# Seven block products for eight: q and k of one 512-token chunk, with their token sums, and the gate folded into v's products

## The chip, the cores and the metric

One core of a Trainium2 chip. The engines work side by side, each through its own instructions in order: TensorE (PE; its weight loads are shown as PEld), VectorE (DVE), ScalarE (ACT), GpSimd (POOL) and SyncE (SP), which here issues the DMAs. They wait for each other by semaphores. The metric is device time in microseconds.

## The reference

Input x is 2048 tokens by 448. The result mixes local attention (16 heads of 28, each token looking at 8 keys, 2 apart) with a two-layer perceptron (1792 hidden, squared ReLU), by a gate per token:

```
g = sigmoid((x * gate_w).sum(-1, keepdims=True))
qkv = x @ wqkv                      # q, k, v: 448 columns each
logits = einsum(q, k[idx]) * scale  # idx = pos - 0, 2, .. 14; masked below 0
a = softmax(logits) @ v[idx] @ wo
h = relu(x @ w1 + b1);  b = (h * h) @ w2 + b2
return g * a + (1 - g) * b
```

All is float32, and all of it is computed.

## The kernel before

**Products.** A float32 matrix is split into a high part, rounded to the type that TensorE reads (`fp32r`), and a low part, the rest: ScalarE writes the high part, VectorE subtracts it (`split_full`). A product is three passes: high by high, high by low, low by high. The contraction of 448 is three blocks of 128 and one of 64. Nearly all products run as two of 64 rows side by side (`side_by_side`, line 186): one on rows 0-63 into one PSUM bank, one on rows 64-127 into another. After a bank's products on one half of the rows it changes to the other half. At this *turn* a one-element write into the bank (VectorE's memset, line 196, in `turn`) waits for the products so far, and the next products wait for it.

**q, k, v.** The tokens come in four chunks of 512 (four tiles of 128). Chunk 0 goes through `qkv_first`, chunks 1 to 3 through `qkv_two`, twice each, two tiles at a time: 63 pairs of products, q of one tile beside k of the other. Its last tuple of steps says after how many pairs a turn is issued and after how many a bank is copied out:

```
[(24, [], (q0, k1)), (36, [], (q1, k0)), (42, [], (v0, v1)), (45, [(0, t0, q0), (1, t1, k1)]),
 (51, [], *beside[:1]), (54, [(0, t1, q1), (1, t0, k0)]), (57, [], *beside[1:]),
 (63, [(2, t0, v0), (2, t1, v1)])]
```

So a bank turned after 24 pairs is written again from pair 36, one turned after 36 from pair 45, one turned after 42 from pair 54. ScalarE copies a finished bank to a staging tile (line 205; three buffers), SP stores that to `q_d`, `k_d` or `v_d` in DRAM (line 211). Chunks 0 and 1 are the first half of the tokens for attention, 2 and 3 the second.

**Attention** works in eight units (two halves, four groups of four heads) from `q_d`, `k_d`, `v_d`. GpSimd multiplies (lines 335 and 342; 8 and 8 instructions a unit) into one of four product buffers (`pp`), and VectorE sums each up (lines 336, 350), at least two products behind.

**The perceptron** takes the chunks in the order 3, 0, 1, 2; its first products lie among the last of chunk 3's v. w1 and w2 are split in pieces. The later pieces of w1 (2 and 3) and w2 are split by `split_copied`: ScalarE writes the high part (line 514) and copies the raw rows to a PSUM bank that is used for that alone (line 515), VectorE subtracts (line 520), 1.3 us later in the kernel's clock; the next copy waits for that. Chunk 3's x tiles are copied to the tiles that the perceptron reads (line 736).

**What sets the order.** The order of instructions is written by a planner inside the kernel. `clock["pe"]` goes on by 203 ns for every pair of 448 columns (`advance`). Work is queued with a due time (`when`: absolute; `at`: from now; `soon`: 1.5 us from now) and is issued on its engine once the clock has passed it; within one `advance` all that is due comes first, then attention's steps (2.3 us for each product with k, the first 17 us after chunk 1's end). Each engine then works through its list in that order, at whatever time the chip gets there. A tile or bank that is used again makes its first writer wait for the last reader of what it held, a DMA's landing included; of the buffers of one kind the one that was given back first is used first.

**The gate.** VectorE multiplies each chunk's raw x by `gate_w` as four instructions (`z_product`), transposes and sums (`z_sums`); the sums go through DRAM once (`z_store`, `z_load`, `z_last`).

Of the kernel before, what the change touches and what calls it, by code (L numbers as in the profile page):

```python
# [14 lines left out]
P = 128  # L15
# [3 lines left out]
G = 4  # L19
# [4 lines left out]
NQ = D + 2  # L24
NZ = 64
NP = 512
# [31 lines left out]
def gated_mix_kernel(ctx: ExitStack, tc: tile.TileContext, xT, wqkv, w1, w2, wo, b1, b2, out):  # L58
# [11 lines left out]
    z_d = tc.dram_tile([P, NZ], F32, name="z_d")  # L70
# [10 lines left out]
    w1h = const.tile([P, 3, F], F32R, name="w1h")  # L81
    w1l = const.tile([P, 3, F], F32R, name="w1l")
# [8 lines left out]

    xpool = ctx.enter_context(tc.tile_pool(name="xpool", bufs=1))
# [5 lines left out]
    zg = smallp.tile([P, 6, NS], F32, name="zg")  # L98
    zt, gt, g1t = zg[:, 0:2], zg[:, 2:4], zg[:, 4:6]
# [36 lines left out]
    def x_split(raw, x, k):  # L136

        split_full(raw[:, k], x.h[k], x.l[k])
# [15 lines left out]
    wqh = ap.tile([P, 3, NP + 2 * D], F32R, name="wqh")  # L154
    wql = ap.tile([P, 3, NP + 2 * D], F32R, name="wql")

    w7h = ap.tile([P, NP + D], F32R, name="w7h")
    w7l = ap.tile([P, NP + D], F32R, name="w7l")
# [3 lines left out]
    nc.gpsimd.memset(halo0, 0.0)  # L162

    stage = {}

    def block(b):

        o = (0, NP, NP + D)[b]
        return slice(o, o + D)
# [29 lines left out]
    def qkv_evacuate(pt, c, tl, b):  # L199
        par, t = c // 2, (c % 2) * 4 + tl  # L200
        first = (b, t // 2) not in stage
        if first:
            stage[b, t // 2] = xap.tile([P, G, 2, C], F32, tag="stage", name=f"st{c}_{tl}_{b}", bufs=ST_BUFS)
        st = stage[b, t // 2]
        nc.scalar.activation(st[:, :, t % 2], pt[:, :D].rearrange("p (g c) -> p g c", g=G), AF.Copy)  # L205
        if not first:
            stage.pop((b, t // 2))
            t0 = t - t % 2
            dst, off = ((q_d, 0), (k_d, HALO), (v_d, HALO))[b]
            dd = dst[par, :, off:off + SP].rearrange("g (p s) c -> p g s c", s=NS)[:, :, t0:t0 + 2]  # L210
            nc.sync.dma_start(dd.rearrange("p g s c -> p g (s c)"), st.rearrange("p g s c -> p g (s c)"))
# [9 lines left out]
    def last(x, acc, tl, b):  # L221

        sl = slice(tl * P, tl * P + P)
        n = block(1) if b == 2 else slice(0, D)
        h, l = w7h[:, n], w7l[:, n]
        return [(acc, x.x7[:, sl], h), (acc, x.x7[:, sl], l), (acc, x.x8[:, sl], h)]

    def accs(c, b, tls, tags):
        return [Acc(t, f"qkv{c}_{tl}_{b}", D) for t, tl in zip(tags, tls)]
# [60 lines left out]


# [101 lines left out]
    def gates(par):  # L393

        e = smp.tile([P, 32], F32, tag="e", name=f"e{par}")[:, :NS]
        nc.scalar.activation(e, zt[:, par], AF.Exp, scale=-1.0)
# [127 lines left out]
    def w1_piece(i, dt, gap):  # L524
# [4 lines left out]
        sl = slice(i * n, (i + 1) * n)  # L529

        def part(k):
            if k < 3 and i > 1:
                split_copied(dt + k * gap, raw[:, k, :n], [(slice(0, P), slice(0, n), w1h[:, k, sl], w1l[:, k, sl])])
                return
            if k < 3:
                split_full(raw[:, k, :n], w1h[:, k, sl], w1l[:, k, sl], soon)
# [12 lines left out]
            for rows, cols, hi, lo in parts:  # L549
                split_full(raw[rows, 3, cols], hi, lo, soon)  # L550
# [10 lines left out]
    def x_load(c):  # L561
        raw = raw_tile(f"xraw{c}")
# [22 lines left out]
    def h_full(x, acc, f, ks):  # L585
        fs = slice(f * P, f * P + P)
        return sum((three(acc, w1h[:, k, fs], w1l[:, k, fs], x.h[k], x.l[k]) for k in ks), [])
# [11 lines left out]
    def h_turn(accs, f):  # L599
        touch(w1h[:, 2].rearrange("p (f n) -> p f n", n=P)[:, f:f + 2, 0:1])  # L600
        for a in accs:
            a.rows = None
# [34 lines left out]
    raws = [raw_tile("wqraw0")]  # L637
    rx = raw_tile("xraw0")
    for k in range(4):
        if k < 3:  # L640
            nc.sync.dma_start(raws[0][:, k, :NQ], wqkv[0, :, k])
        else:
            for b, rows in ((0, slice(0, 64)), (1, slice(64, P))):
                nc.sync.dma_start(raws[0][rows, k, :NQ], wqkv[b, rows, k])
# [3 lines left out]
    for b, tag in ((1, "k"), (2, "v")):  # L648
        raw = attp.tile([P, 3, D], F32, tag=tag, name=f"wqraw{b}")
        for k in range(3):  # L650
            nc.sync.dma_start(raw[:, k], wqkv[b, :, k, :D])
        raws.append(raw)
    raw7 = attp.tile([P, D], F32, tag="q", name="wqraw7")
    nc.sync.dma_start(raw7, wqkv[2, :, 3, :D])
    x = x_tiles(0, xap)
    for k in range(3):
        nc.scalar.activation(wqh[:, k, :D], raws[0][:, k, :D], AF.Copy)
# [7 lines left out]
        nc.vector.tensor_sub(wql[:, k, :D], raws[0][:, k, :D], f32(wqh[:, k, :D]))  # L665
        for cols in halves:
            nc.vector.tensor_sub(x.l[k][:, cols], rx[:, k, cols], f32(x.h[k][:, cols]))
    split_full(raws[0][:, 3, :D], w7h[:, :D], w7l[:, :D])
    split_x78(rx[:, 3], x.x7, x.x8)

    zs = smp.tile([P, 3, NZ], F32, tag="lg", name="zs")
    zu = xcp.tile([P, CH], F32, tag="zu", name="zu")
    zpart, zall, gw = zs[:, 0], zs[:, 1], zs[:, 2, 0:4]
    nc.vector.tensor_copy(gw, raws[0][:, :, D])

    def z_product(raw, k):

        r = slice(0, P if k < 3 else 64)
        if k:
            nc.vector.scalar_tensor_tensor(zu[r], raw[r, k], gw[r, k:k + 1], zu[r], op0=ALU.mult, op1=ALU.add)  # L680
        else:
            nc.vector.tensor_scalar_mul(zu, raw[:, 0], gw[:, 0:1])

    def z_sums(c):

        nc.vector.transpose(zu, zu)
        nc.vector.tensor_reduce(
            zpart.rearrange("p (b c t) -> p c t b", b=4, c=4)[:, c],
            zu.rearrange("p (t b r) -> p t b r", t=4, b=4), axis=AX.X, op=ALU.add)

    def z_store():

        nc.sync.dma_start(z_d, zpart)

    def z_load():

        for b in range(4):
            nc.sync.dma_start(
                zall[b * 32:b * 32 + 32].rearrange("p (a n) -> p a n", a=4),
                z_d[:, b * 16:b * 16 + 16].rearrange("(a c) n -> c a n", a=4))  # L700

    def z_last():

        nc.vector.tensor_reduce(
            zt.rearrange("p q s -> p (q s)"), zall.rearrange("p (a n) -> p n a", a=4), axis=AX.X, op=ALU.add)

    def wq_split(b, k):
        if k < 3:
            split_full(raws[b][:, k], wqh[:, k, block(b)], wql[:, k, block(b)])
        else:  # L710
            split_full(raw7, w7h[:, NP:], w7l[:, NP:])
# [9 lines left out]

    def x_begin(c):
# [6 lines left out]
        if c == 1:  # L729
            xs[c] = X(own, [prodp.tile([P, W * C], F32R, tag="pp", name=f"x{c}_3{n}", bufs=PP_BUFS)[:, 48:48 + CH]  # L730
                            for n in range(2)])
            return
        xm[c] = x_tiles(c, xpool)
        xs[c] = X(own + xm[c].t[3:])
        for j in range(3):
            at(12000.0 + j * 2000.0, lambda j=j: nc.scalar.activation(xm[c].t[j], f32(own[j]), AF.Copy))
# [16 lines left out]
    for k in range(4):  # L753
        when(15000.0 + k * 700.0, z_product, rx, k)
    when(17900.0, z_sums, 0)
    when(60500.0, z_store)
    when(76000.0, z_load)
    when(86500.0, z_last)
    for c, t in SPLIT_AT.items():
        when(t, x_begin, c)  # L760
        for k in range(4):
            when(t + k * 900.0, lambda c, k: x_split(xraw[c], xs[c], k), c, k)
            when(t + k * 900.0 + 450.0, lambda c, k: z_product(xraw[c], k), c, k)
        when(t + 4200.0, z_sums, c)
        if c < 3:
            when(t + 4500.0, x_more, c + 1)
            when(t + 5000.0, lambda c: x_spill(c, xs[c]), c)
    when(10500.0, x_spill, 0, x)
# [3 lines left out]
    when(67000.0, w1_piece, 2, 77400.0, 1450.0)  # L772
    when(68000.0, w1_piece, 3, 83300.0, 1450.0)
    when(70000.0, biases)
    when(86000.0, w2_piece, 0, 4, 93000.0, 1400.0)
    when(89600.0, w2_piece, 4, 3, 100200.0, 1400.0)
# [16 lines left out]
    for c in range(4):  # L793
        x = xs[c]
        if c == 0:
            qkv_first(x)
        else:
            qkv_two(x, c, 0, copies=c == 3)
            qkv_two(x, c, 2, (mlp_one, mlp_two) if c == 3 else (), c == 3)
        if c == 1:  # L800
            st_["spilled"] = 0
            clock["on"] = True
            clock["att"] = clock["pe"] - 1.0
            advance(0.0)
        if c == 3:
            st_["spilled"] = 1
# [414 lines left out]
```

## Time and profile before

| what | value |
|---|---|
| median of 3 runs | 413.61 us (413.28 to 413.69) |
| the profiled execution: span from the first to the last instruction | 412.0 us |
| TensorE busy | 407.8 us, 3835 matmuls |
| VectorE, ScalarE, GpSimd busy | 270.6, 210.4, 268.4 us |
| DMA | 73.83 MB, mean 179 GB/s |
| granted TensorE clock | 1.0 in all 40 slices of the span |

The profiled execution's own time is its span; the runs' times hold some 1.6 us more, which lie around it. A row of the timeline has its start and length in us, the engine, the line, the operation with output and inputs, how many instructions were merged into it, and in brackets how long the engine was idle before and what released it. A row of the groups ends with busy time in us, the mean of one in ns, and the idle time before with its releasers. A row of TensorE's waits has the waiting group, what it waited for, the total, the count and the longest. A DMA's row on SP's queue is its issue; how long after that it landed is a line of its own.

### The profile page before, as it was taken

How to read it: one execution, taken by the hardware profiler on the slowest of the kernel's cores; microseconds unless marked ns; L12 is line 12 of the kernel's file. 1: busy time of each engine (PE TensorE's matmuls, PEld its weight loads, DVE VectorE, ACT ScalarE, POOL GpSimd, SP SyncE). 2: the span in 40 equal slices, each digit the busy share in tenths (PEclk: the TensorE clock that was granted, in tenths of full speed). 3: DMA queues.
4: the chain of work that ended last, by engine and by line, in shares of the span. 5: the costliest groups of instructions: out<-in, count | busy, mean ns of one | idle time of the engine just before them, and what ended most of it. 6: DMA issues, size and time to landing. Idle time of an engine off the chain costs nothing.

```text
span 412.0 us, 9331 instructions
## 1 busy us (share of the span) xinstructions
PE 407.8 (99%) x3835; PEld 366.0 (89%) x3835; DVE 270.6 (66%) x430; ACT 210.4 (51%) x461; POOL 268.4 (65%) x167
## 2 busy tenths in 40 slices
PE   8999999999999999999999999999999999999997
PEld 7999999999888888888888888989898888888996
DVE  4590745276767766787656798879576677892354
ACT  4641646387775555444565535444653254346540
POOL 0000001955999999989989899999899977940000
PEclk9999999999999999999999999999999999999999
DMA  7999999979262315654112649765146530168304
GB/s 213 368 351 309 286 390 288 355 223 315 91 241 99 128 51 209 208 186 152 41 47 105 222 158 270 196 146 154 28 157 200 217 130 2 45 179 132 95 0 181
DMA packets 66763, 73.83 MB, mean 179 GB/s; under 512 B 33120, under 2 KB 59296, under 8 KB 66464
## 3 DMA queue, kind: packets, MB, share of 16 engines
q1 hardware_dynamic: 66720, 73.23, 55.4%
q8 instruction: 30, 0.49, 0.5%
q14 instruction: 13, 0.11, 0.1%
HBM read 45.74 MB, written 28.28 MB: 180 GB/s over the span
## 4 chain that ended last, share of the span: by engine, by line
PE 99%; DVE 0%; issue 0%
PE b L186 33%; PE h L186 32%; PE qkv L186 23%; PE a L186 7%; PE qkv L255 2%; PE warm L634 1%; PE a L993 1%; PE last L993 0%; DVE bt L872 0%; PE last L985 0%; PE a L985 0%; DVE zero L631 0%; DVE b1z L632 0%
## 5 line engine op out<-in xcount | busy, mean ns | idle before, releaser
L335 POOL TENSOR_TENSOR qk<-q,k 128x896 f32<-128x896 f32 x64 | 135.2, 2144 | 84.2 <-DMA k<-k_d 76.0
L342 POOL TENSOR_TENSOR av<-lg,v 128x896 f32<-128x896 f32 x64 | 119.2, 1957 | 6.2 <-DVE lg L336 5.6
L621 DVE TENSOR_TENSOR h<-h,h 128x512 fp32r<-128x512 f32 x56 | 38.4, 688 | 66.8 <-ACT h L624 66.5
L186 PE MATMUL qkv<-wqh,x 64*128 64x448 f32 x528 | 78.2, 359 | 0.0
L336 DVE TENSOR_REDUCE lg<-qk 128x32 f32<-128x896 f32 x64 | 67.0, 1074 | 0.0
L350 DVE TENSOR_REDUCE o<-av 128x112 f32<-128x896 f32 x64 | 66.4, 1070 | 0.1
L186 PE MATMUL b<-w2ah,h 64*128 64x448 f32 x448 | 66.3, 359 | 0.0
L186 PE MATMUL b<-w2bh,h 64*128 64x448 f32 x448 | 66.1, 359 | 0.0
L622 ACT ACTIVATE h<-h,b1z 128x512 f32<-128x512 f32 x56 | 36.7, 655 | 43.6 <-PE h L186 43.6
L186 PEld LDWEIGHTS qkv<-wqh,x 64*128 64x128 f32 x528 | 49.4, 184 | 3.6
L186 PE MATMUL qkv<-wql,x 64*128 64x448 f32 x264 | 47.7, 358 | 0.0
L186 PEld LDWEIGHTS b<-w2bh,h 64*128 64x128 f32 x448 | 42.1, 184 | 3.5
L186 PEld LDWEIGHTS b<-w2ah,h 64*128 64x128 f32 x448 | 42.0, 184 | 3.7
L205 ACT ACTIVATE st<-qkv 128x448 f32<-128x448 f32 x48 | 23.5, 542 | 34.3 <-PE qkv L186 31.7
L186 PE MATMUL b<-w2bl,h 64*128 64x448 f32 x224 | 40.7, 358 | 0.0
L186 PE MATMUL b<-w2al,h 64*128 64x448 f32 x224 | 40.5, 358 | 0.0
L623 ACT ACTIVATE h<-h 128x512 fp32r<-128x512 f32 x56 | 33.5, 598 | 1.7
L624 ACT ACTIVATE h<-h 128x512 f32<-128x512 f32 x56 | 33.3, 594 | 0.0
L573 ACT ACTIVATE h<-h 128x4 fp32r<-128x4 f32 (+1 forms) x35 | 7.2, 207 | 44.4 <-PE b L186 44.2
L186 PE MATMUL h<-x2b,w1h 64*128 64x512 f32 x168 | 28.1, 386 | 0.0
L186 PE MATMUL h<-x,w1h 64*128 64x512 f32 x168 | 28.1, 386 | 0.0
L186 PE MATMUL h<-x1b,w1h 64*128 64x512 f32 x168 | 28.1, 386 | 0.0
(150 smaller groups left out, 688.6 us busy)
## 6 DMA issues: line engine op xcount, KB each, us to landing
k<-k_d SPq DMA_DIRECT2D x8, 840.0 KB, 5.6
v<-v_d SPq DMA_DIRECT2D x8, 840.0 KB, 5.0
x_d<-x SPq DMA_DIRECT2D x11, 512.0 KB, 6.8
q_d<-st SPq DMA_DIRECT2D x8, 448.0 KB, 5.5
k_d<-st SPq DMA_DIRECT2D x8, 448.0 KB, 5.2
v_d<-st SPq DMA_DIRECT2D x8, 448.0 KB, 5.8
w1raw<-w SPq DMA_DIRECT2D x4, 896.0 KB, 9.2
q<-q_d SPq DMA_DIRECT2D x8, 448.0 KB, 3.6
```

Source lines behind the costliest of these rows:

```text
L186: nc.tensor.matmul(acc.pt[:, :acc.n], a[rows], w[rows], start=acc.todo == acc.all, stop=acc.todo == 1)
L205: nc.scalar.activation(st[:, :, t % 2], pt[:, :D].rearrange("p (g c) -> p g c", g=G), AF.Copy)
L255: nc.tensor.matmul(acc.pt[:, :D], a, w, start=k == j == 0, stop=False)
L335: nc.gpsimd.tensor_mul(pr, q[:, s:s + 1].to_broadcast([P, W, C]), k[:, s:s + W])
L336: pending.append(lambda: nc.vector.tensor_reduce(lg[:, s], pr.rearrange("p w (h d) -> p w h d", h=HG), axis=AX.X, op=ALU.add))
L342: nc.gpsimd.tensor_mul(pr.rearrange("p (h d) w -> p w h d", h=HG), lg[:, s][:, :, :, None].to_broadcast([P, W, HG, DH]), v[:, s:s + W].rea ...
L350: nc.vector.tensor_reduce(o[:, g * C:(g + 1) * C], pr, axis=AX.X, op=ALU.add)
L573: nc.scalar.activation(ap, f32(ap), AF.Copy)
L621: nc.vector.tensor_sub(hl, pt, f32(hh))
L622: ops += [lambda pt=pt, r=r: nc.scalar.activation(pt, pt, AF.Relu, bias=b1t[:, f + r:f + r + 1]), lambda pt=pt, hh=hh: nc.scalar.activatio ...
L623: lambda pt=pt, hh=hh: nc.scalar.activation(hh, pt, AF.Square),
L624: lambda pt=pt, r=r, low=low: (nc.scalar.activation(pt, pt, AF.Square), at(delays[r], low))]
```

## The change

- **Chunk 2's q and k by seven block products.** The four tiles make two groups (`Group`) of two tiles. In a group the blocks are: two tiles, two 64- or 128-row blocks of the contraction, and q and k as the two column blocks. Instead of the eight block products of a 2 by 2 by 2 product it takes seven of sums (Strassen's way, in the form with few additions), for blocks 0 and 1 (128 rows) and for the first part of the third with the odd block; a remainder (`rest`) is done as it was. Group 0 works on rows 0-63 while group 1 works on 64-127, then the other way round. Banks: `x` takes products 1, 6 and 7, `z` takes 5 and 3, `y` takes 2, `w` takes 4. ScalarE copies x or z out between (`copied`), VectorE adds the others onto the staging tile (`added`).
- **Weight sums** (`weight_sums`): 22 steps on VectorE and ScalarE, due from 17.0 us each 0.9 us, in place on the raw weights; the results lie where w2's first half comes later.
- **Token sums** (`token_sums`): chunk 2's raw tokens are loaded by four DMAs to the four `pp` buffers of attention's products and summed there, in six steps due from 46.1 us each 0.9 us; the last two cut the sums in high and low parts, three instructions of each kind a step, into tiles `e0` to `e3`.
- **Tiles.** w1 is now two halves of columns, the second in six tiles `e0` to `e5` (`halfp`), which hold q's raw weights first, then the token sums and (`e4`) the staging tile of group 1's k. v's staging tiles of chunk 2 lie in `pp`. x1's last block lies in `xpool`.
- **The gate** is a column of v's products: 450 columns for 448, and a one-column copy on ScalarE for each tile; the z functions go.
- **Times moved.** w1's pieces 2 and 3, the biases and w2's pieces are due 1.8 us earlier; chunk 3's copies for the perceptron (`x_copies`) are due 3, 5 and 7 us after chunk 3 begins (before: 12, 14 and 16 us after 53.5).

```diff
+    def qkv_seven(c, x, inner):
+        two = [Group(c, u, x) for u in range(2)]
...
+        v = V(c, x, (0, 1), inner)
+        v.first()
+        first(1)
+        v.second()
+        first(2)
+        second(1)
+        each("copied", 1, 0, 0)
+        first(5)
+        second(2)
+        other(2, 0, 0)
+        each("added", 2, 0, 0)
+        second(5)
+        each("copied", 5, 1, 1)
+        first(6)
+        first(4)
+        second(6)
+        each("copied", 6, 1, 0)
+        other(3, 0, 1)
+        second(3, True)
+        second(4)
+        first(7)
+        other(4, 1, 0)
+        v = V(c, x, (2, 3), inner)
+        v.first()
+        second(7)
+        each("copied", 7, 0, 1)
+        each("added", 4, 0, 1, True)
+        first(3, False)
+        each("added", 3, 1, 0)
+        v.second()
+        other(7, 1, 1)
+        each("added", 7, 1, 1, True)
```

In it `first(n)` is 6 pairs and, but for the last, a turn; `second(n)` and `other` are 3 pairs each; `v.first()` is 12 pairs and a turn, `v.second()` 9 pairs and the copying out. The functions below it:

```diff
+        def stage(self, b):
+            if self.st[b] is None:
+                if b == self.u == 1:
+                    t = halfp.tile([P, FA], F32, tag="e4", name=f"st{self.c}_{self.u}_{b}")
+                    self.st[b] = t.rearrange("p (g s c) -> p g s c", g=G, s=2)
+                else:
+                    self.st[b] = stage_tile(f"st{self.c}_{self.u}_{b}")
+            return self.st[b]
+        def copied(self, n, b, r):
+            nc.scalar.activation(self.stage(b)[:, :, r], heads(self.to(n).pt), AF.Copy)
+        def added(self, n, b, r, store=False):
+            st = self.stage(b)
+            nc.vector.tensor_add(st[:, :, r], heads(self.to(n).pt), st[:, :, r])
+            if store:
+                stage_store(st, self.c // 2, (self.c % 2) * 4 + 2 * self.u, b)
...
+    def w1_second():
+        for n in range(2):
+            for k in range(3):
+                w1b[n][k] = halfp.tile([P, FA], F32R, tag=f"e{3 * n + k}", name=f"w1b{'hl'[n]}{k}")
...
+        def cut(j):
+            split_full(raw[j], *(t[:, :CH] for t in sums[c, j]), soon)
+            for u, rows in enumerate((LOW, HIGH)):
+                split_full(raw[2 + j][rows, u * 2 * P:(u + 1) * 2 * P], *(t[rows, CH:] for t in sums[c, j]), soon)
+        return made(0) + made(2) + [lambda: (begin(), cut(1)), lambda: cut(0)]
...
-    when(67000.0, w1_piece, 2, 77400.0, 1450.0)
-    when(68000.0, w1_piece, 3, 83300.0, 1450.0)
+    steps(17000.0, 900.0, weight_sums())
+    when(46000.0, lambda: steps(46100.0, 900.0, token_sums(2)))
+    when(65200.0, w1_piece, 2, 75600.0, 1450.0)
+    when(66200.0, w1_piece, 3, 81500.0, 1450.0)
...
-    for c in range(4):
-        x = xs[c]
...
+    qkv_seven(2, xs[2], True)
+    x_copies(3)
+    x = xs[3]
+    qkv_two(x, 3, 0, copies=True)
+    qkv_two(x, 3, 2, (mlp_one, mlp_two), True)
```

More of the change, by code (lines that the diff above doesn't have):

```diff
@@ L228, in accs @@
     def accs(c, b, tls, tags):
[L229 removed]
+        return [Acc(t, f"qkv{c}_{tl}_{b}", NV if b == 2 else D) for t, tl in zip(tags, tls)]
     def run(c, todo, steps):
@@ new lines, in beside, with turned, weights @@
+    def beside(low, high):
+        assert len(low[1]) == len(high[1])
+        for a in range(0, len(low[1]), 3):
+            for i in range(a, a + 3):
+                for bank, prods in (low, high):
+                    bank.add(*prods[i])
+            advance(3 * MM448)
+    def turned(*banks):
+        for bank in banks:
+            nc.vector.memset(bank.pt[0:1, 511:512], 0.0)
+    def weights(b, j):
+        if j < 3:
+            return wqh[:, j, block(b)], wql[:, j, block(b)]
+        return w7h[:, D:D + NV], w7l[:, D:D + NV]
@@ new lines, in qkv_seven, with first, second, other @@
+    def qkv_seven(c, x, inner):
+        two = [Group(c, u, x) for u in range(2)]
+        def first(n, turn=True):
+            beside(*(g.first(n) for g in two))
+            if turn:
+                turned(*(g.to(n) for g in two))
+        def second(n, turn=False):
+            beside(*(g.second(n) for g in two[::-1]))
+            if turn:
+                turned(*(g.to(n) for g in two))
+        def other(n, r, b):
+            beside(*(g.rest(n, r, b) for g in two[::-1]))
+        def each(f, *a):
+            for g in two:
+                getattr(g, f)(*a)
+        v = V(c, x, (0, 1), inner)
[30 more added lines that the diff above has]
+        each("added", 7, 1, 1, True)
@@ new lines, in gated_mix_kernel, with __init__, prods, first @@
+    class V:
+        def __init__(self, c, x, tls, inner):
+            self.c, self.x, self.tls, self.inner = c, x, tls, inner
+            self.banks = [Bank(f"v{c}_{tl}", "b", NV) for tl in tls]
+        def prods(self, i, rows, js):
+            sl = slice(self.tls[i] * P, self.tls[i] * P + P)
+            return self.banks[i], sum((passes(*(tuple(v[rows] for v in o) for o in (
+                (self.x.h[j][:, sl], self.x.l[j][:, sl]), weights(2, j)))) for j in js), [])
+        def first(self):
+            beside(*(self.prods(i, rows, range(4)) for i, rows in enumerate((LOW, HIGH))))
+            turned(*self.banks)
+        def second(self):
+            beside(*(self.prods(i, rows, range(3)) for i, rows in ((1, LOW), (0, HIGH))))
+            for bank, tl in zip(self.banks, self.tls):
+                qkv_evacuate(bank.pt, self.c, tl, 2, self.inner)
@@ L561, in x_load @@
     def x_load(c):
+        if c == 2:
+            rows = [prodp.tile([P, W * C], F32, tag="pp", name=f"xraw{c}_{k}", bufs=PP_BUFS)[:, :CH] for k in range(4)]
+            for k in range(4):
+                nc.sync.dma_start(rows[k], xT[c, :, k])
+            return rows
         raw = raw_tile(f"xraw{c}")
@@ L585, in h_full @@
     def h_full(x, acc, f, ks):
-        fs = slice(f * P, f * P + P)
-        return sum((three(acc, w1h[:, k, fs], w1l[:, k, fs], x.h[k], x.l[k]) for k in ks), [])
+        return sum((three(acc, w1_f(0, k, f), w1_f(1, k, f), x.h[k], x.l[k]) for k in ks), [])
     def h_last(x, acc, f):
@@ L599, in h_turn @@
     def h_turn(accs, f):
-        touch(w1h[:, 2].rearrange("p (f n) -> p f n", n=P)[:, f:f + 2, 0:1])
+        if f == NFA - 1:
+            for r in range(2):
+                touch(w1_f(0, 2, f + r)[:, 0:1])
+        else:
+            half = w1_rows(0, 2)[f // NFA].rearrange("p (f n) -> p f n", n=P)
+            touch(half[:, f % NFA:f % NFA + 2, 0:1])
         for a in accs:
@@ new lines, in token_sums, with r, made, begin @@
+    def token_sums(c):
+        raw = xraw[c]
+        add, sub = nc.vector.tensor_add, nc.vector.tensor_sub
+        def r(j, i):
+            return raw[j].rearrange("p (u t n) -> p u t n", u=2, t=2)[:, :, i]
+        def made(a):
+            one, two = a, a + 1
+            return [lambda: (add(r(two, 1), r(two, 1), r(one, 1)), sub(r(one, 1), r(one, 0), r(one, 1))),
+                    lambda: (sub(r(one, 0), r(two, 1), r(one, 0)), sub(r(two, 0), r(two, 0), r(one, 0)))]
+        def begin():
+            for j in range(2):
+                sums[c, j] = [halfp.tile([P, FA], F32R, tag=f"e{2 * j + n}", name=f"s{c}_{j}{'hl'[n]}")[:, 48:48 + CH + 2 * P]
+                              for n in range(2)]
+        def cut(j):
[3 more added lines that the diff above has]
+        return made(0) + made(2) + [lambda: (begin(), cut(1)), lambda: cut(0)]
@@ L722, in x_begin, with steps @@
+    def steps(t, gap, fns):
+        for i, fn in enumerate(fns):
+            when(t + i * gap, fn)
     def x_begin(c):
```

257 lines of the change are left out of this document (161 added, 96 removed).

## The prediction

> **What bounds the kernel now.** I read the page first (span, busy shares), then the chain that ended last in order of time, then TensorE's waits.
>
> ```profile
> span 412.0 us, 9331 instructions
> PE 407.8 (99%) x3835; PEld 366.0 (89%) x3835; DVE 270.6 (66%) x430; ACT 210.4 (51%) x461; POOL 268.4 (65%) x167
> PE 99%; DVE 0%; issue 0%
> ...
> 4.34 8.87 PE qkv L255 x36
> 13.21 91.55 PE qkv L186 x912
> ...
> 119.13 2.72 PE h L186 x24
> ...
> PE warm L634 <- DVE b1z L632: 1.2, 1, 1.2
> ```
>
> TensorE is the chain from end to end, and once started it never waits for another engine: the one wait is before the warm-up. So 912 products of 64 rows took 91.55 us, 0.2008 us for a pair (one product on rows 0-63, one on 64-127, side by side). Each pair taken out is worth that, and each new wait of TensorE is paid in full, because no later gap can swallow it. The sum below goes against this execution's 412.0 us span; the median of the runs is 413.61, 1.6 more, and I add the differences to that.
>
> **The gain.** In the third chunk q and k take 168 products now. By seven, each of the two token pairs has 7 x 6 (two row blocks of 64, three passes), 7 x 3 and 4 x 3 for the odd block: 75, so 150 in all; v keeps 84. 18 products fewer are 9 pairs: 9 x 0.2008 = 1.81 us. The gate adds two columns to v's products: pairs of 512 columns take 2.72 / 12 = 0.2267 us, so a column costs (226.7 - 200.8) / 64 = 0.40 ns, and 168 pairs of v pay 168 x 2 x 0.40 ns = 0.14 us. Net **-1.67 us**.
>
> **Off TensorE, early.** Added on VectorE: 11 differences of weights and 11 low parts (22 x 0.62), 8 sums of tokens, 6 low parts, 6 more turn memsets, 8 additions that end q and k; ScalarE gains 17 high parts and 16 one-column copies of the gate, and has 6 evacuations for 8. Removed on VectorE: four chunks of gate work.
>
> ```profile
> L680 DVE SCALAR_TENSOR_TENSOR zu<-xraw,zs,zu 128x512 f32<-128x512 f32 x8 | 6.0, 746 | 0.1
> ...
> L520 DVE TENSOR_TENSOR w2al<-copy,w2ah 128x448 fp32r<-128x448 f32 x7 | 4.4, 630 | 3.3 <-ACT copy L515 3.2
> ...
> L573 ACT ACTIVATE woh<-woh 128x1 fp32r<-128x1 f32 x7 | 1.3, 192 | 1.5 <-PE a L186 1.5
> ```
>
> Per chunk that was some 0.5 + 3 x 0.75 + 0.7 + 0.7 = 4.1 us, so the weight sums, one each 0.9 us, replace about as much up to 42 us, and I price them at nothing; their cover is the 6 to 12 pairs (1.2 to 2.4 us) that lie between a turn and the pair that needs it. If it were gone, one turn late by one 0.62 us low part would cost at most that. SP loses five gate transfers and one spill and gains two weight loads and three of tokens, all ahead of need: nothing.
>
> **First new wait, in the third chunk's opening.** The last two steps of `token_sums` cut in the kernel's clock at 49.7 and 50.6 us, while the second chunk ends at (36 + 90 + 126) x 0.203 = 51.16 (on the chip 13.21 + 216 x 0.2008 = 56.58 us). Their six high parts so stand on ScalarE ahead of the second chunk's last evacuation and of x3's first high part.
>
> ```profile
> 54.86 0.98 ACT L205 ACTIVATE st<-qkv 128x448 f32<-128x448 f32 x2 [0.77 <-PE qkv L186]
> 56.71 0.98 ACT L205 ACTIVATE st<-qkv 128x448 f32<-128x448 f32 x2 [0.87 <-ACT st L205]
> 57.72 2.19 ACT L115 ACTIVATE x<-xraw 128x512 fp32r<-128x512 f32 x4
> ...
> 7.66 0.72 ACT L664 ACTIVATE x<-xraw 128x256 fp32r<-128x256 f32 x2 [0.84 <-DMA xraw<-xT]
> ...
> 58.38 0.69 DVE L116 TENSOR_TENSOR x<-xraw,x 128x512 fp32r<-128x512 f32 x1 [5.91 <-DMA v_d<-halo]
> ```
>
> From 55.84, when the evacuation of 54.86 is done, two cuts of 0.53 + 2 x 0.31 us end at 58.15; the evacuation with two gate columns (0.98 + 0.2; one such copy is 192 ns, partly overlapped) at 59.35; x3's first high part at 59.98; VectorE's low part of it at 60.6. It stands ahead of the turn of v's banks (x3 begins at 53.5, twelve pairs into the chunk), so that ends at 60.7, and v's second half is due after 18 pairs, at 56.58 + 3.61 = 60.19. **+0.55 us**. Bounds: 0 (ScalarE 0.5 us quicker), 0.9 (the small instructions not overlapped).
>
> I went through the chunk's other turns and bank reuses the same way: each has 6 pairs or more, with VectorE empty at it or one 0.62 us instruction ahead, and the banks that the fourth chunk begins in were freed 12 pairs before the seam. Nothing.
>
> **Second new wait, in the fourth chunk's first half.** This is what I take to decide. There VectorE barely keeps up now:
>
> ```profile
> 83.83 0.62 DVE L520 TENSOR_TENSOR w1l<-copy,w1h 128x448 fp32r<-128x448 f32 x1 [5.06 <-ACT copy L515]
> 84.37 1.07 DVE L336 TENSOR_REDUCE lg<-qk 128x32 f32<-128x896 f32 x1
> 85.36 0.61 DVE L520 TENSOR_TENSOR w1l<-copy,w1h 128x448 fp32r<-128x448 f32 x1
> 86.59 0.62 DVE L520 TENSOR_TENSOR w1l<-copy,w1h 128x448 fp32r<-128x448 f32 x1 [0.61 <-ACT copy L515]
> 87.13 1.08 DVE L336 TENSOR_REDUCE lg<-qk 128x32 f32<-128x896 f32 x1
> 88.20 0.06 DVE L196 MEMSET qkv<- 1x1 f32 x2
> 88.32 1.13 DVE L520 TENSOR_TENSOR w17l<-copy,w17h 64x128 fp32r<-64x128 f32 x4
> 89.37 1.07 DVE L336 TENSOR_REDUCE lg<-qk 128x32 f32<-128x896 f32 x1
> 90.38 0.64 DVE L520 TENSOR_TENSOR w1l<-copy,w1h 128x448 fp32r<-128x448 f32 x1
> 90.44 0.06 DVE L196 MEMSET qkv<- 1x1 f32 x2
> ```
>
> The seam is at 13.21 + 342 x 0.2008 = 81.88 us. The first turn (88.2) is due after 36 pairs, at 89.1; the second (90.44) after 45, at 90.9. Slack 0.9 and 0.4 us.
>
> The change puts three things there. (1) Group 1's k is staged in tile `e4`, and `e4` becomes w1's low part k = 1: VectorE may not write that until the store of k has landed. (2) The last two additions (2 x 0.6 us), behind an attention reduce. (3) The three copies of x3, which lie in an idle stretch of ScalarE now, come 3, 5 and 7 us after the seam, among the w1 copies that feed VectorE.
>
> ```profile
> 95.69 0.37 SPq L211 DMA_DIRECT2D q_d<-st  x1
> 96.15 0.61 SPq L211 DMA_DIRECT2D k_d<-st  x1
> 97.00 0.56 SPq L211 DMA_DIRECT2D v_d<-st  x1
> ...
> DMA to landing us min/median/max: 2.8/2.8/2.8
> DMA to landing us min/median/max: 3.8/3.8/3.8
> DMA to landing us min/median/max: 4.6/4.6/4.6
> k_d<-st SPq DMA_DIRECT2D x8, 448.0 KB, 5.2
> ...
> 68.47 0.74 SPq L211 DMA_DIRECT2D k_d<-st  x1
> DMA to landing us min/median/max: 7.9/7.9/7.9
> ...
> 70.48 2.95 ACT L736 ACTIVATE x<-x 128x1024 fp32r<-128x1024 f32 x3
> 86.58 1.22 ACT L514 ACTIVATE w17h<-w1raw 64x128 fp32r<-64x128 f32 x4
> ...
> 70.89 12.59 POOL L335 TENSOR_TENSOR qk<-q,k 128x896 f32<-128x896 f32 x6 [69.51 <-DMA k<-k_d]
> ```
>
> Without the first wait, which shifts all of it alike, the seam comes at 56.58 + 117 x 0.2008 = 80.07. POOL's first product is long done, so its reduce, emitted 9 pairs earlier, runs 79.5 to 80.55; the additions end at 81.15 and 81.75. Stores go out at about 80.75 (v), 81.2 and 81.75 (k of groups 0 and 1). Three stores of this size in a row landed after 2.8, 3.8 and 4.6 us (95.69 to 97.00, each tile's landing asked in its own window); the store of 68.47, among w1's loads, after 7.9. I take the third, 4.6, since this store is the third of a burst too: 86.35. VectorE: low part 0 at 82.6, a reduce at 83.65, then low part 1 waits and ends at 86.95. Queued behind it by the kernel's clock are two reduces (products at 77.355 and 79.655, the turn at 79.779): 89.0, then the turn, 89.15. TensorE needs it at 80.07 + 36 x 0.2008 = 87.30: **+1.85 us**.
>
> Then low part 2 (89.75), the one copy bank refilled by ScalarE (0.55: 90.3), four w17 low parts (1.13: 91.5), a reduce (92.55), the next turn 92.65; due nine pairs after 89.15, at 90.96: **+1.7 us**. The turn of v follows one low part later and is in time, and from there VectorE has the idle time of the next half. With the landing at 2.8 us the first of these is 0.05 and the second still 1.7, since the copies of x3 hold the w17 parts back; with 7.9 us the pair is 1.85 + 3.3 + 1.7 = 6.85.
>
> A sentence of the Trainium skill bears on it: "DMA: Bandwidth & Descriptors", section "Anatomy of one DMA", has a DMA's semaphore wait for the last byte's receipt, some 2 us besides the bytes, fitted for the GpSimd path. An estimate from that page is 2.0 + 0.459 MB / 436 GB/s = 3.05 us for one store, with which the sum would be 414.5 instead; the trace agrees for the first store of a burst (2.8), not for the third (4.6).
>
> POOL: its fifth product takes the buffer of v's stage and waits for v's store, so the first unit ends near 92.4 instead of 90.4, and unit 1 starts some 2 us later; TensorE by then is later by more, and POOL's order is paced by it, so I take nothing.
>
> **Sum.** 413.61 - 1.67 + 0.55 + 1.85 + 1.7 = **416.0 us**, slower by 0.6%. Its own range: 414.7 (no first wait, landing after 3.8) to 417.0 (first wait 0.9, landing after the median 5.2).
>
> **Rivals.**
> - Everything is hidden: 413.61 - 1.67 = 411.9, faster. One mechanism decides: whether the turn after 36 pairs gets behind the landing. If k's store were down by 83.65, VectorE would run through and turn at 86.6, 0.7 us before need; ScalarE would further have to feed the w17 copy 1.3 us sooner than I have it. For it: the whole early part is covered, and TensorE has not one wait now. Against: 83.65 is 1.9 us after the store goes out, and the shortest landing quoted is 2.8. Chance 0.24.
> - The landing is early, but the copies of x3 and the extra cuts still cost 1.3 to 2 us: 413.2 to 414.0, no change. Speaks for it the 2.8 us row; against it the burst. 0.17.
> - The store meets loads still under way and takes 7.9 us: 413.61 - 1.67 + 0.55 + 6.85 = 419.3. For it, the waiting reduces then stop POOL as well; against it, w1's loads would by then be issued earlier than now, as no third-chunk store stands ahead of them on SP. 0.05.
> - My forecast: 0.54.
>
> No difference that a measurement of this kernel can tell is one within 0.2% (412.8 to 414.4). Faster 0.24, same 0.17, slower 0.59. The range that leaves out under 2 in 10 reaches from the hidden case, 411.8, to 417.4.
>
> **What would show it.** TensorE 18 matmuls fewer, v's with 450 columns. In TensorE's waits: one on VectorE's memset or low part near 60 us of about half a us, and two near 87 and 91 us of 1 to 2 us each; before them, VectorE idle for 2 to 3 us ahead of a w1 low part, released by the transfer k_d<-st. If VectorE is not idle there, or TensorE's waits list stays empty, I am wrong and the time is 411.9. If ScalarE's copies are what VectorE waits for, the second rival holds.

## The result, and the profile after

| | before | after |
|---|---|---|
| median of the runs on the same chip | 413.44 us (413.10 to 413.69) | 425.77 us (424.43 to 427.52) |
| ratio, 95% interval | | 1.0305 (1.0277 to 1.0333) |
| span of the profiled execution | 412.0 us | 423.4 us |

The change made the kernel 3% slower. The prediction had the sign and the places of two waits, but 2.4 us where it is 12.3. The page, first its totals, then the granted clock in 40 slices, then the chain that ended last:

```profile
span 423.4 us, 9362 instructions
PE 411.9 (97%) x3817; PEld 395.8 (93%) x3817; DVE 279.2 (66%) x454; ACT 220.2 (52%) x498; POOL 267.2 (63%) x167
...
PEclk9999999989989999999999999999999999999999
...
PE 87%; ACT 4%; DMA 3%; DVE 2%; POOL 1%; issue 1%; SPq 1%; ACTq 0%; POOLq 0%; DVEq 0%
```

The 18 matmuls are gone (3835 to 3817), yet TensorE is busy for longer, since two slices of the clock are no longer full; and the chain, 99% TensorE before, passes through DMA, ScalarE and VectorE. TensorE's waits (total, count, longest), where before there was only the one of the warm-up:

```profile
PE qkv L201 <- DVE qkv L211: 3.2, 1, 3.2
PE h L201 <- ACT w1ah L799: 2.4, 1, 2.4
PE warm L864 <- DVE b1z L862: 1.2, 1, 1.2
PE v L334 <- DVE v L350: 0.9, 1, 0.9
PE b L201 <- DVE h L851: 0.4, 1, 0.4
PE h L201 <- ACT st L233: 0.3, 1, 0.3
```

**The wait of 3.2 us** is the one foreseen at `e4`. The chain's row for the store and VectorE's timeline:

```profile
83.42 6.08 DMA k_d<-st
```

```profile
83.89 1.08 DVE L553 TENSOR_REDUCE lg<-qk 128x32 f32<-128x896 f32 x1
89.58 0.62 DVE L737 TENSOR_TENSOR w1bl<-copy,w1bh 128x448 fp32r<-128x448 f32 x1 [4.62 <-DMA k_d<-st]
90.13 2.07 DVE L553 TENSOR_REDUCE lg<-qk 128x32 f32<-128x896 f32 x2
92.13 0.64 DVE L737 TENSOR_TENSOR w1bl<-copy,w1bh 128x448 fp32r<-128x448 f32 x1
92.19 0.06 DVE L211 MEMSET qkv<- 1x1 f32 x2
```

VectorE stands still for 4.62 us until the store has landed, then does the two reduces and the low part that are queued behind, and only then the turn; TensorE, which had run out of pairs at 89.09, starts again at 92.33.

**The wait of 2.4 us** was not foreseen. It begins on SP. In order, SP's issues, then one row each of GpSimd, VectorE, ScalarE and TensorE:

```profile
101.20 0.36 SPq L225 DMA_DIRECT2D q_d<-st  x1
101.65 0.46 SPq L225 DMA_DIRECT2D k_d<-st  x1
102.16 0.89 SPq L777 DMA_DIRECT2D w2raw<-w  x1
103.15 1.22 SPq L523 DMA_DIRECT2D q<-q_d  x1
104.42 0.47 SPq L524 DMA_DIRECT2D k<-k_d  x1
```

```profile
111.85 6.21 POOL L552 TENSOR_TENSOR qk<-q,k 128x896 f32<-128x896 f32 x3 [16.41 <-DMA k<-k_d]
```

```profile
114.00 1.08 DVE L553 TENSOR_REDUCE lg<-qk 128x32 f32<-128x896 f32 x1 [5.44 <-POOL qk L552]
```

```profile
115.65 0.55 ACT L732 ACTIVATE copy<-w2raw 128x448 f32<-128x448 f32 x1 [4.34 <-DVE w2al L737]
116.13 0.19 ACT L799 ACTIVATE w1ah<-w1ah 128x2 fp32r<-128x2 f32 x1
```

```profile
116.38 0.75 PE L201 MATMUL h<-x,w1ah 64*128 64x512 f32 x2 [2.35 <-ACT w1ah L799]
```

Before, attention's second unit loaded its q and k ahead of the fourth chunk's stores (95.69 us) and of w2's second load (97.61), and GpSimd began that unit 15 us earlier:

```profile
90.46 0.34 SPq L306 DMA_DIRECT2D q<-q_d  x1
90.85 0.42 SPq L307 DMA_DIRECT2D k<-k_d  x1
```

```profile
96.89 6.33 POOL L335 TENSOR_TENSOR qk<-q,k 128x896 f32<-128x896 f32 x3 [6.45 <-DMA k<-k_d]
```

Now the loads stand behind those stores and behind w2's second load, and go out at 103.15. The staging and this are one rule: a queue does things in the order in which the planner emitted them. Attention's steps kept their due times, while the third chunk became 1.8 us shorter and all that follows it came some 1.8 us earlier by the kernel's clock (w2's loads, by their due times in the kernels, 2.0 us), past them. GpSimd then starts its second unit at 111.85, VectorE waits in front of a reduce, w2's low part waits behind the reduce, ScalarE's next copy waits for that low part, and the perceptron's turn (line 799) waits behind the copy.

**The clock.** Behind each of the two waits TensorE runs at half its clock for some 3.4 us. The view of windows, set to the stretches around the two waits (length, TensorE's busy time and matmuls, granted clock, DMA share, GB/s):

```profile
89.10:92.60 3.50, 0.27 (x2) 0.99 0.01 2
92.60:96.00 3.40, 3.40 (x20) 0.50 0.38 89
113.00:116.50 3.50, 1.15 (x13) 0.99 0.00 0
116.50:119.90 3.40, 3.40 (x17) 0.50 0.02 5
```

By the starts of its matmuls a pair of 448 columns takes 0.37 us there instead of 0.20.

Where the 11.4 us of span went, by the starts of TensorE's stages in the two traces (the chunks' borders of before, which its rows don't name, at 0.2006 us a pair):

| stage | after less before |
|---|---|
| start of the 64-row pairs (12.94 for 13.14 us) | -0.2 |
| first two chunks (450-column pairs of v) | +0.25 |
| third chunk: 25.16 us for 25.27, where 9 pairs fewer are -1.8 | -0.1 |
| fourth chunk up to the first h: 28.19 for 22.87; wait 3.4, half clock 1.8 | +5.3 |
| first h to the first b: 16.89 for 11.97; wait 2.5, half clock 1.7, second wait 0.5 | +4.9 |
| from there to the end: 293.3 for 292.1 | +1.2 |

### The profile page after: what moved, and what is told of

It is laid out like the page before. It is cut to its first block, busy times and chain, and to the rows that moved or that the text cites. A ratio compares the mean times of both kernels' runs of the same rounds, so it can differ in the third digit from the quotient of the medians.

```text
span 423.4 us, 9362 instructions
## 1 busy us (share of the span) xinstructions
PE 411.9 (97%) x3817; PEld 395.8 (93%) x3817; DVE 279.2 (66%) x454; ACT 220.2 (52%) x498; POOL 267.2 (63%) x167
## 4 chain that ended last, share of the span: by engine, by line
PE 87%; ACT 4%; DMA 3%; DVE 2%; POOL 1%; issue 1%; SPq 1%; ACTq 0%; POOLq 0%; DVEq 0%
PE b L201 31%; PE h L201 30%; PE qkv L201 11%; PE a L201 7%; PE qkv L281 2%; DMA k<-k_d 2%; POOL qk L552 1%; DMA k_d<-st 1%; PE v L334 1%; ACT st L233 1%; PE x L334 1%; ACT copy L732 1%; PE z L334 1%; PE warm L864 1%; PE a L1247 1%
## 5 line engine op out<-in xcount | busy, mean ns | idle before, releaser
L201 PE MATMUL b<-w2ah,h 64*128 64x448 f32 x448 | 74.8, 359 | 0.0
L201 PE MATMUL qkv<-wqh,x 64*128 64x448 f32 (+1 forms) x384 | 63.0, 368 | 3.2 <-DVE qkv L211 3.2
L201 PEld LDWEIGHTS b<-w2ah,h 64*128 64x128 f32 x448 | 59.3, 184 | 0.3
L201 PEld LDWEIGHTS b<-w2bh,h 64*128 64x128 f32 x448 | 56.0, 184 | 1.6 <-DVE h L851 0.7
L201 PE MATMUL b<-w2al,h 64*128 64x448 f32 x224 | 55.1, 358 | 0.0
L201 PE MATMUL b<-w2bl,h 64*128 64x448 f32 x224 | 52.7, 359 | 0.0
L201 PE MATMUL qkv<-wql,x 64*128 64x448 f32 (+1 forms) x192 | 46.7, 367 | 0.0
L201 PEld LDWEIGHTS b<-w2al,h 64*128 64x128 f32 x224 | 34.6, 184 | 0.1
L201 PEld LDWEIGHTS b<-w2bl,h 64*128 64x128 f32 x224 | 32.4, 184 | 0.3
L201 PEld LDWEIGHTS qkv<-wql,x 64*128 64x128 f32 x192 | 26.9, 188 | 0.5
```

The costliest lines, as they stand in the source:

```text
L201: nc.tensor.matmul(acc.pt[:, :acc.n], a[rows], w[rows], start=acc.todo == acc.all, stop=acc.todo == 1)
```

## The experiments

Each is the changed kernel with the edit shown, unless it says otherwise. The kernel before ran at 413.3 to 413.4 us (medians) on the same chips.

**One wait at a time, and both.** The first takes the staging tile away from w1: the tile x2 of the perceptron's copies is idle in the third chunk. The third copy of x, which fills that tile, is due 2 us later for it.

```
-  t = halfp.tile([P, FA], F32, tag="e4", ...)
+  t = xpool.tile([P, 2 * CH], F32, tag="x2", ...)[:, :2 * D]
-  at(3000.0 + j * 2000.0, ...)                # x_copies
+  at((3000.0, 5000.0, 9000.0)[j], ...)
```

> Group 1's k is staged in the free tile x2 of the MLP's copies instead of in w1's low part k = 1; everything else is as changed. Theory (two separate causes: the staging tile, and SP's order): TensorE's wait of 3.2 us near 89 us goes, and the 3.4 us of halved clock behind it (some 1.8 us lost), so 425.8 - 5.2 = 420.6; unit 1's q and k still stand behind the fourth chunk's first stores on SP, POOL's second unit still begins about 9 us late against TensorE, and the wait near 114 us moves to about 109 us and stays above 2 us, with the halved clock behind it. Rival (one cause: the stall makes POOL late): without the stall unit 1 is loaded in time and the second wait goes too: 425.8 - 10.1 = 415.7. Rival (the additions and the copies of x hold VectorE up by themselves): a wait of 1 to 2 us stays near 87 to 91 us, and the time is 422 or more.

Measured: 421.57 us (ratio to before 1.0187, 1.0158 to 1.0215), span 419.7. The first wait falls to 0.5 us, and the halved clock near 93 us is gone. The second wait stays and is longer. TensorE's waits and SP's issue of unit 1's q:

```profile
PE h L201 <- ACT w1ah L799: 3.3, 1, 3.3
...
PE qkv L201 <- DVE qkv L211: 0.5, 1, 0.5
```

```profile
98.28 0.89 SPq L777 DMA_DIRECT2D w2raw<-w  x1
99.26 1.22 SPq L523 DMA_DIRECT2D q<-q_d  x1
```

So the second wait is not a consequence of the first: without a stall ahead of it the load still stands behind the stores and w2's load. The time is 1 us above the 420.6 expected: the second wait is 0.9 us longer than in the changed kernel, and 0.5 us of the first is left.

The second edit is one constant, with the staging as in the change:

```
-ATT_DELAY = 17000.0
+ATT_DELAY = 15200.0
```

> Attention begins 1.8 us earlier by the kernel's clock (17.0 to 15.2 us after the second chunk), as much as everything else behind the third chunk was moved; the staging tile stays. Theory: unit 1's q and k are issued on SP ahead of the fourth chunk's stores, right behind POOL's last product of unit 0 (near 95 us instead of 103), POOL's second unit begins near 101 us instead of 112, and TensorE's wait of 2.4 us and the halved clock behind it (together 4.9 us) go: 425.8 - 4.9 = 420.9; the wait for k's store stays at 3 to 4 us. Rival (one cause: the stall makes POOL late): POOL stays late, both waits stay, 424 to 426.

Measured: 420.31 us (1.0159, 1.0115 to 1.0202), span 418.3. SP issues the load ahead of the stores, GpSimd starts 11 us sooner, and the wait of the perceptron's turn is gone:

```profile
93.19 0.46 SPq L523 DMA_DIRECT2D q<-q_d  x1
93.69 0.42 SPq L524 DMA_DIRECT2D k<-k_d  x1
100.46 0.37 SPq L225 DMA_DIRECT2D q_d<-st  x1
```

```profile
100.85 6.31 POOL L552 TENSOR_TENSOR qk<-q,k 128x896 f32<-128x896 f32 x3 [8.17 <-DMA k<-k_d]
```

The wait at the staging tile is there, but as two waits, the second 9 pairs behind the first:

```profile
90.60 0.48 PE L201 MATMUL qkv<-wqh,x 64*128 64x448 f32 x2 [2.20 <-DVE qkv L211]
...
94.99 0.47 PE L201 MATMUL qkv<-wqh,x 64*128 64x448 f32 x2 [2.32 <-DVE qkv L211]
```

This is the pair of waits that the prediction drew (1.85 and 1.7 us). The first is shorter than the 3.24 us of the changed kernel, since one reduce and not two stands behind the store on VectorE. In the changed kernel the halved clock behind the first wait hid the second: VectorE's memsets for the two turns stand 3.4 us apart there (92.19 and 95.58), and nine pairs take 1.8 us at full clock but 3.4 at half. Here the clock stayed full after the first wait and fell after the second.

Both edits together:

> Both edits at once: group 1's k in the tile x2, attention 1.8 us earlier. Theory: both waits and both stretches of halved clock go, 425.8 - 10.1 = 415.7, and 1 us less if the tail's loss hangs on attention's lateness: 414.5 to 415.7; what is left over before is the wait of 1 us in the third chunk's opening, and the stretch of 18 fewer products is eaten by it and by the slower 450-column pairs. Rival (a third cause, the copies of x among w1's copies): a wait of 1 to 2 us stays near 89 to 91 us: 417 or more.

Measured: 414.77 us (1.003, 1.0017 to 1.0044), span 412.6, the clock full throughout. Of the 12.3 us, 11.0 are gone; the two edits alone took 4.2 and 5.5. They are not independent: the first leaves one wait of 3.3 us, the second two of 2.2 and 2.3, and in the profiled execution of either one stretch of halved clock is left. The tail's loss goes with the second edit too: from the first b product to TensorE's last matmul it is 293.3 and 293.2 us with GpSimd late (the change, the first edit), 292.3 in the other two, 292.1 before. The waits left over are that of the third chunk's opening, 0.9 us, and this one:

```profile
90.81 0.47 PE L201 MATMUL qkv<-wqh,x 64*128 64x448 f32 x2 [0.42 <-DVE qkv L211]
```

**The copies of x.** The seven products undone, all else of the change kept:

```
-qkv_seven(2, xs[2], True)
+qkv_two(xs[2], 2, 0)
+qkv_two(xs[2], 2, 2)                 # and w1's and w2's due times 1.8 us later
```

> The seven products are undone in the third chunk (q and k by rows as in the other chunks, no staging in a weight tile), and the times of w1 and w2 put back by 1.8 us; the gate in v's products, the sums of weights and of tokens, the tokens' loading and the later copies of x stay. Theory: the time is that of before plus the two columns of v's pairs (0.4 to 0.6 us): 413.9. Rival (the copies of x, 3 to 7 us into the fourth chunk, cost a wait by themselves): 415 to 416.

Measured: 415.76 us (1.0052, 1.0039 to 1.0066), the rival's number. TensorE waits for the turn after 45 pairs of the fourth chunk, and on ScalarE two copies of x lie among w1's parts ahead of it:

```profile
91.81 0.47 PE L201 MATMUL qkv<-wqh,x 64*128 64x448 f32 x2 [1.07 <-DVE qkv L211]
```

```profile
84.92 1.05 ACT L996 ACTIVATE x<-x 128x1024 fp32r<-128x1024 f32 x1
85.87 0.56 ACT L731 ACTIVATE w1bh<-w1raw 128x448 fp32r<-128x448 f32 x1
86.34 0.53 ACT L732 ACTIVATE copy<-w1raw 128x448 f32<-128x448 f32 x1
86.80 1.05 ACT L996 ACTIVATE x<-x 128x1024 fp32r<-128x1024 f32 x1
```

A second execution of it, profiled once:

> The kernel with the seven products undone, once more on this chip, for its profile beside the next: TensorE's wait of 1.1 us near 91 us is there again, 413.6 us of span.

The same wait of 1.07 us, at 93.21; but the span was 416.1. Its first x transfer landed 1 us later, and the 64-row pairs began at 14.65 us instead of 12.44. The opening alone moves single executions of these kernels by 2 us, so below whole times are compared by their medians only.

Both edits, and the copies of x at 9.5, 11.5 and 13.5 us behind the third chunk:

> As with both edits (k in the tile x2, attention 1.8 us earlier), and the three copies of x moved from 3, 5 and 9 us to 9.5, 11.5 and 13.5 us behind the third chunk's end. Theory: the wait of 0.6 us that TensorE still has near 90 us comes from the copies on ScalarE ahead of w17's high parts; with them gone from there the low parts come 2 us sooner, the turn is in time, and the span falls by 0.5 to 0.6 us: 412.6 to 412.0 (times 414.8 to 414.2). Rival: VectorE's own load (two additions more than before) makes the turn late: the wait stays, 414.8.

Measured: 414.75 us, unchanged (1.0032, 1.002 to 1.0045). The wait near 90 us is gone, so the copies were its cause; but the third copy now lies ahead of w2's first part on ScalarE, and a turn 11 us later pays:

```profile
102.04 0.47 PE L201 MATMUL qkv<-wqh,x 64*128 64x448 f32 x2 [0.23 <-DVE qkv L211]
```

**The third chunk's opening.** On top of that, the token sums 3.7 us earlier:

```
-when(46000.0, lambda: steps(46100.0, 900.0, token_sums(2)))
+when(42300.0, lambda: steps(42400.0, 900.0, token_sums(2)))
```

> As the one before, and the sums of tokens and their cuts 3.7 us earlier by the kernel's clock (steps from 42.4 us instead of 46.1). Theory: ScalarE is idle from 48.9 to 52.9 us and takes the cuts there, the second chunk's last evacuation and x3's high part are no longer behind them, and TensorE's wait of 0.9 us (1.1 us with the slower pairs beside it) near 60 us goes: span 410.9 us, time 412.5 to 413.1, within 0.3% below the kernel before: of the 1.8 us of the 18 products, 0.5 to 0.6 is eaten by v's 450-column pairs. Rival: the cuts collide with the weight parts that ScalarE and VectorE cut near 46 to 50 us, and another turn of the second chunk is late: no gain against the run before, 414.

Measured: 413.48 us (1.0012, 0.9999 to 1.0024), 1.27 below the run before it. The wait near 60 us is gone. 413.48 is 0.4 above the upper end expected, and not told from the kernel before by its interval.

**The version with no wait, and what the parts are worth in it.** The copies of x at 6.5, 9.5 and 11.5 us:

> As the kernel with both edits and the earlier token sums, the copies of x at 6.5, 9.5 and 11.5 us behind the third chunk's end instead of 9.5, 11.5 and 13.5. Theory: the last pause that is left (0.4 us near 100 us: the third copy lay ahead of w2's first high part on ScalarE, so VectorE's low part and the turn behind it were late) goes, and no turn near 90 us gets late, as one copy costs 1 us there and that turn had 0.9 us to spare: 413.48 - 0.5 = 413.0, at the edge of what can be told from the kernel before. Rival: the first copy makes the turn after 45 pairs late again by 0.3 us or more: 413.3 to 413.6.

Measured: 412.75 us (0.9986, 0.9976 to 0.9997). TensorE's list of waits is again that of the kernel before:

```profile
PE warm L864 <- DVE b1z L862: 1.2, 1, 1.2
```

It is the fastest kernel that computes all of the reference, ahead of the kernel before by 0.14%, at the edge of what these runs can tell. The same with the third chunk's q and k by rows:

> The same placement of everything, but the third chunk's q and k by rows, as in the other chunks (no seven products; w1's and w2's times put back by 1.8 us; the sums of weights and tokens are still made, and not used). Theory: what the seven products bring by themselves is the 18 products, 1.81 us, with each new wait taken away: 413.0 + 1.8 = 414.8, that is 1.4 us above the kernel before, for v's wider pairs and for what the sums cost. Rival: the seven products bring less than the count (their banks' many turns, 42 wider pairs at 0.206 instead of 0.202 us): 413.4 to 414.2.

Measured: 414.83 us (1.0033, 1.0021 to 1.0045). The seven products bring 2.1 us by the medians. In the two profiled executions the third chunk by itself takes 23.62 us with them and 25.49 without, 1.87 less, where the count of 18 products gives 1.81. All else in the change (the gate in v's products, the sums, the loading) costs 1.4 us against the kernel before, without any wait. By the starts of the stages it is spread: some 0.3 us in each of the four chunks and 0.4 behind them. The wait of 1.07 us that the version with the copies at 3, 5 and 7 us had is gone, and the time is 0.93 us below its 415.76. The width of v's pairs was tried alone:

> As the first of these, but v's products are 448 columns wide and the gate is left out (its place is filled from v's first column, so that all other work stays). Theory: the two columns cost far more than the 0.14 us of the prediction: by the starts of the pairs 0.0019 us each for 84 pairs of the first two chunks, 0.0061 for 42 of the third and 0.002 to 0.003 for 42 of the fourth, 0.5 us in all, so 0.5 us less than the first of these. Rival (the columns cost what the count says, 168 x 2 x 0.40 ns): 0.14 us less, which can't be told from nothing.

Measured: 412.52 us, 0.23 less. In the two profiled executions the stretch from the first 64-row pair to the first h product is 90.13 us without the columns and 90.51 with them, 0.38 more. With a spread of 1 us and more among the runs of either, 0.14 and 0.5 aren't told apart, and what makes up the rest of the 1.4 us stays open.

**The halved clock by itself.** The kernel before, with pauses of TensorE in its second and third chunk:

```
+for _ in range(n): nc.vector.memset(acc.pt[:, 448:512], 0.0)   # ahead of the 7th and 34th pair, n = 8 .. 22
```

> The kernel before, with eight pauses of TensorE put into its second and third chunk: 8 to 22 memsets of 128x64 on the bank in use, on VectorE, ahead of the 7th and the 34th pair of each half, each pause longer than the last (some 1 to 3 us). It prices the halved clock by itself. Theory (the clock is decided by the idle share of a fixed window of 3.413 us, between 39% and 56% by the runs so far): a pause of 2 us or more that lies in one window is followed by 3.413 us at 0.5, and a shorter one, or one split by a window's border, is not; each such stretch adds some 1.7 us to the pauses' sum. Rival (only a pause of about a whole window, over 3 us, halves the clock): at most the last pause does. Time 430 to 436 either way.

Measured: 454.79 us in one run. The pauses came out longer than meant (1.66 to 5.07 us, 27.7 in all), so the expected time was missed by 19 us; the question is answered all the same, by this one execution. Windows of 3.4 us by the clock's own steps, two with a pause of 2.12 us in the first, then three around a pause of 3.26 us that lies across a border:

```profile
39.60:43.00 3.40, 1.28 (x14) 1.00 0.96 322
43.00:46.40 3.40, 3.40 (x22) 0.50 0.01 3
```

```profile
78.67 0.47 PE L186 MATMUL qkv<-wqh,x 64*128 64x448 f32 x2 [3.26 <-DVE qkv L288]
```

```profile
73.70:77.10 3.40, 1.71 (x18) 1.00 0.93 307
77.10:80.50 3.40, 1.83 (x18) 1.00 1.01 336
80.50:84.00 3.50, 3.50 (x40) 1.00 0.95 392
```

The pause of 2.12 us halved the clock, the one of 3.26 us did not. All changes of the clock in this run, as in every other trace here, lie a whole number of 3.413 us apart. Sorted by the idle share of one such window at full clock, over this run and the two-wait run of the second edit: 35, 37, 39, 45 and 50% idle were followed by full clock, 56, 62, 69, 71, 83, 88 and 100% by half. These two windows are the nearest below and above in the second edit's run (39% and 56%):

```profile
89.70:93.10 3.40, 2.08 (x18) 1.00 0.01 2
93.10:96.50 3.40, 1.51 (x14) 1.00 0.76 230
96.50:99.90 3.40, 3.40 (x22) 0.50 1.04 426
```

The run prices the halved clock too. Its span is 41.0 us longer than that of the kernel before. The pauses are 27.7 of them; TensorE worked for 24.5 us at half its clock, and half of that, 12.3 us, is what it lost. The two make 40.0.

## Why the prediction was wrong, step by step

- **The 18 products.** Right: 1.81 us expected, 2.1 between the medians of the two versions without waits, 1.87 in the third chunk itself.
- **v's columns.** 0.14 us expected; by the starts of the stages some 0.4, by the medians of the run without them 0.2. Not settled, and small.
- **Third chunk's opening.** Right in place and cause, short in size: 0.55 us expected (0 to 0.9), 0.94 idle, and 1.27 between the medians when it was taken away. The two cuts took 2.8 us on ScalarE, not 2.3.
- **The store in `e4`.** Right in mechanism; the size was off: 1.85 us expected, 3.24 measured. The third chunk's end came at 81.67 us, 1.05 later than worked out, but that moves the store and the turn's need alike. The term that was too small is the landing: 6.08 us after the store's issue began, not 4.6. Of that the issue itself is 1.38 us on SP, where the row of 4.6 that the prediction took has 0.56. The estimate that the prediction made from the Trainium skill's page "DMA: Bandwidth & Descriptors", section "Anatomy of one DMA", 3.05 us for one store, is further off; the measurement decides.
- **The second turn.** 1.7 us expected, none in the changed kernel, because the halved clock ahead of it made the nine pairs in between last longer. It stood in the run of the second edit, where the clock stayed full between the two: 2.32 us. There a copy of x (1.04 us) lies on ScalarE ahead of the w17 parts, as the prediction had it. What the runs tested of that cause is the 0.42 us that both edits left: with the copies moved away it went.
- **The steps that failed: the queue.** "SP ... all ahead of need: nothing" and, of POOL, "unit 1 starts some 2 us later ... I take nothing". GpSimd's second unit started 15 us later. The prediction went through SP's added DMAs but not through the ones that others moved past: the shorter chunk moved its successors' stores and w2's load past attention's load, which stayed. That is one constant's worth: with attention 1.8 us earlier the kernel falls by 5.5 us.
- **The step that failed: the price of a wait.** That "each new wait of TensorE is paid in full" took a wait's length for its whole price; the profile before shows no wait and a full clock. In the changed kernel two waits were followed by a stretch of 3.413 us at 0.5 each, in which, by the pairs' starts, 1.8 and 1.7 us more were lost. The Trainium skill, "TensorE: Matmul & The Clock Gate", section "What's actually happening", has a free-running window of 3413 ns after which an idle TensorE drops to half its clock; the traces agree to the digit (3.413). The Trainium skill's advice on the same page, in section "Why this matters for your kernels", to allow no idle gap above some 3 us, is not what these runs show: 1.92 us idle inside one window was enough, and a gap of 3.26 us across a border halved nothing.

Among the rivals, the store that takes 7.9 us (419.3) came nearest, mostly for other reasons. The range failed because it was built from the waits that the change adds on VectorE alone, each at its bare length.

## What to carry to other kernels

When a stage under a planner gets shorter, list what is due by that stage's clock and what by another: whatever did not move along has changed places in some queue, and a DMA queue that never waited before is where to look first. A tile lent to a store is given back at the store's landing, so look for the engine that writes it next and what is queued behind that write. Count a new wait of TensorE of 2 us or more as up to 1.8 us dearer than its length; and after taking the waits away, measure what the change is worth bare: here 2.1 us of gain against 1.4 us of upkeep.

## What the runs showed of the hardware that was not expected

By the steps of the granted clock in these traces, it is decided per window of 3.413 us on a grid that stays fixed within an execution. At full clock a window up to 50% idle kept it full, one from 56% halved the next window; what lies between was not met. In a halved window the demand is higher: 16% idle brought the full clock back, 37%, 50% and 78% (all in the run with pauses) kept it at half for another window. So the same wait can cost its length, or its length and 1.8 us, by where it falls on the grid: the waits of 2.20 and 2.32 us above cost one halved window between them, not two.

The times of the other runs hint at the same. One halved window is 0.004 of a span of some 420 us (1.7 of 420). Of the changed kernel's four runs, the two at a mean granted clock of 0.991 and 0.992 took 424.4 and 425.2 us, the two at 0.987 and 0.988 took 426.3 and 427.5. Of the second edit's four, the one at 1.0 took 418.4 us, those at 0.994 to 0.996 420.1 to 422.5. It is no more than a hint: of the first edit's four, the one at 0.992 was no longer than the three at 0.996.
